# A top-k attention and channel-mix kernel: keys and queries stored as head, d, token

## The chip, the core and the metric

The kernel runs on one NeuronCore of a Trainium2 chip. The core has TensorE (PE: matmuls and transposes; its weight loads are listed as PEld), VectorE (DVE), ScalarE (ACT), GpSimd (POOL) and SyncE (SP, which here only issues DMAs). Each engine works through its own list of instructions in order and waits on semaphores for the others. Matmul results land in PSUM; everything else lies in SBUF, which, like PSUM, has 128 partitions. The metric is the device time of one launch in microseconds.

## The reference

Attention over 8 batches, 8 heads, 576 tokens and a head width of 64, in float32, in which each query keeps only its 32 largest scores; then a channel mix over the joined heads (512 channels, 1024 hidden).

```python
scores = scale * np.matmul(q, k.transpose(0, 1, 3, 2))
kth = np.partition(scores, -top_k, axis=-1)[..., -top_k:-top_k + 1]
mask = scores >= kth
scores = np.where(mask, scores, -1000000000.0)
scores = scores - np.max(scores, axis=-1, keepdims=True)
attn = np.exp(scores)
attn = attn / (np.sum(attn, axis=-1, keepdims=True) + 1e-09)
x = np.matmul(attn, v)              # then batch, token, head * d
...
xk = mu_k * x + (1.0 - mu_k) * x_prev
xr = mu_r * x + (1.0 - mu_r) * x_prev
k = np.maximum(xk @ w_k, 0.0)
v = k * k @ w_v
r = 1.0 / (1.0 + np.exp(-(xr @ w_r)))
return (r * v).astype(np.float32)
```

`x_prev` is x shifted by one token within its batch.

## The kernel before

**Tiles and slots.** Two heads make a pair; there are 4 pairs in each of 8 batches. A tile is 128 queries of one head against all 576 keys, the keys in two halves of 288 that stand on the upper and the lower 64 partitions of the key tile `K`. A pair of heads has 9 tiles: for each of four blocks of 128 tokens one tile per head, and a ninth for the last 64 tokens of both heads. A batch is walked in two halves: tiles 0 to 3 of the pairs 0, 1, 2, 3, then tiles 4 to 8 of the pairs 3, 2, 1, 0. Each such walk through a pair is a visit; there are 64 visits and 288 tiles. The key tile of a pair is made on its first visit and kept in one of four homes (`K0` to `K3`) for the second.

`pipeline` emits the program slot by slot, one tile entering in each. A slot n computes the scores of tile n (`scores`, L237, into the PSUM tile `ps`) and copies them to SBUF (`keep`, ACT, L246). One slot later DVE takes the eight largest of each of seven pieces of the row (`candidates`, L270), then the best of these in three rounds (L273, L276). ACT counts the scores over the 24th best (`count`, L286), POOL blanks those (`below`, L289), DVE takes the next eight (L915) and picks the 32nd value (L294). ACT computes the exponentials (L297), DVE masks and sums them (L300), TensorE turns the result (`turn_tile`, L313), ACT copies it (L317), and at the end of every four tiles TensorE multiplies it with v (`weigh`, L365) and DVE places the quotient into x (`place`, L371, L376). The steps of one slot come in the fixed order of the list `ORDER` (L42); a step's place there is its place in each engine's queue.

**Keys and queries before.** In DRAM they lie as batch, head, token, d. TensorE needs them with d on the partitions. So for each head j of a pair `load_keys` brings the keys as 96 tokens x 3 blocks x 2 halves (L178), `turn_k` transposes the three blocks into a PSUM tile (L206) and ACT copies it into `K` one slot later (L214, the place "high", second in the order). Queries come 256 tokens at a time (`load_near`, L172), each twice, so that they stand on both halves of the partitions after the turn; `turn_q` transposes the two blocks and ACT copies them (L209; DVE in the first pair, L221). The last 64 tokens of both heads go the same way through `load_rest` (L185), `turn_rest` and L227. All these PSUM tiles come from the pool `psM` (4 buffers), which the turned tiles and the channel mix use too. Keys are loaded 5 and 4 slots before the pair's first tile, queries 4 and 3 before it, and the turns are in the step `prep`, 4 to 1 slots before it. The first pair has its own `prep_first`, with a step `second` for its second head.

SP issues all DMAs in program order: weights (L120), keys, queries, v (L193, L194: these wait until the last products with the previous v are done) and the finished rows (L467).

**Channel mix.** `mix_steps` hands out the channel mix in pieces, of 3 matmuls with 512 columns or 6 with 256 (`three`, L424 to L426: values are split in a high and a low part). A planner (`Lanes`) decides how many pieces a slot takes: TensorE's account gets `TENSOR` at the end of each slot (L609, not over `CAP`), the attention's steps charge it (0.92 for scores, 0.47 for the turn of a tile, 2.5 for `weigh`, 0.35 for each turn of keys or queries, L859 and L863), and each piece costs `PIECE`. The pieces wait for tokens to be complete, and in the first 215 us also for the weights, which are split into two parts by ACT, DVE and POOL. These numbers only order the program; nothing waits on them on the chip.

A second way through the kernel, `prep_all` and the loop over batches at L976, runs only if a check of the counts fails; it does not run here.

```python
PACE, TENSOR, SHARE, PIECE, CAP, MOST = 4.60, 4.10, 0.74, 0.71, 4.45, 4
...
self.free[lane] = min(self.free[lane] + (TENSOR if lane == "pe" else PACE), CAP)
```

Of the kernel before, what the change touches and what calls it, by code (L numbers as in the profile page):

```python
# [9 lines left out]
F32 = mybir.dt.float32  # L10
# [15 lines left out]
KB, KP = 3, 96  # L26
# [12 lines left out]
PACE, TENSOR, SHARE, PIECE, CAP, MOST = 4.60, 4.10, 0.74, 0.71, 4.45, 4  # L39
END, HASTE = 36, 0.56  # L40
EXPS, EVAC = 3, (0, 'et')
ORDER = """exp high norm evac best0 c0 drop0 c1 best1 c2 drop1 first score turn inv loads keep sign c3 best2 c4 bounds eighth norm2 count et late below act c5 early thr c6 second mask place mix prep weigh dve pool weights""".split()  # L42
# [3 lines left out]
def topk_attention_channel_mix(ctx: ExitStack, tc: tile.TileContext, q, k, v, mu_k, mu_r, w_k, w_v, w_r, out):  # L46
# [112 lines left out]
    def heads(x, batch, hp):  # L159
        return batch(x)[2 * hp:2 * hp + 2]  # L160

    def load_part(g, x, batch, hp, j, tag=None):
        t = g.one.tile([128, NKC, 2, D], F32, name="kq", tag=tag or f"kq{j}")
        for i in range(2):
            nc.sync.dma_start(t[:, :, i, :], heads(x, batch, hp)[j, :MAIN].rearrange("(p c) d -> p c d", c=NKC))
        return t

    def load_near(g, x, batch, hp, j, c0):

        t = g.one.tile([128, 2, 2, D], F32, name="q_near", tag=f"kq{j}")  # L170
        for i in range(2):
            nc.sync.dma_start(t[:, :, i, :], heads(x, batch, hp)[j, c0 * 128:(c0 + 2) * 128].rearrange("(c p) d -> p c d", p=128))  # L172
        return t

    def load_keys(g, batch, hp, j):
        t = g.one.tile([KP, KB, 2, D], F32, name=f"kt{j}")
        for i in range(2):
            nc.sync.dma_start(t[:, :, i, :], heads(k, batch, hp)[j, i * HS:(i + 1) * HS].rearrange("(b p) d -> p b d", p=KP))  # L178
        return t

    def load_rest(g, batch, hp):
        t = g.one.tile([128, 1, 2, D], F32, name="qr_in")
        for j in range(2):
            for i in range(2):
                nc.sync.dma_start(t[j * 64:(j + 1) * 64, 0, i, :], heads(q, batch, hp)[j, MAIN:])  # L185
        return t
# [9 lines left out]
    def flat(ap):  # L196
        return ap.rearrange("p e d -> p (e d)")

    def new_k(g, P):
        P.K = g.one.tile([128, 2, HS], F32, name="K", tag=f"K{P.home}")  # L200

    def turn(pt, x):

        n = x.shape[0]
        for c in range(x.shape[1]):
            nc.tensor.transpose(pt[:, c * n:(c + 1) * n], flat(x[:, c]), ident[:n, :n])  # L206

    def copy_out(fast):
        return nc.vector.tensor_copy if fast else lambda to, x: nc.scalar.activation(to, x, AF.Copy)  # L209

    def turn_k(g, P, j, L):
        pt = g.psM.tile([128, MAIN], F32, name="pk", tag="pm")[:, :HS]
        turn(pt, P.kt[j])
        L.at(1, "high", lambda: nc.scalar.activation(P.K[:, j], pt, AF.Copy))  # L214

    def turn_q(g, P, j, L, fast=False):
        n = P.qt[j].shape[1] * 128
        pt = g.psM.tile([128, MAIN], F32, name="pq", tag="pm")[:, :n]
        turn(pt, P.qt[j])
        P.qs[j] = g.one.tile([128, n], F32, name=f"qs{j}")  # L220
        L.at(1, "high", lambda: copy_out(fast)(P.qs[j], pt))  # L221

    def turn_rest(g, P, L):
        pt = g.psM.tile([128, MAIN], F32, name="pr", tag="pm")[:, :128]
        turn(pt, P.rest)
        P.qr = g.two.tile([128, 128], F32, name="qr")
        L.at(1, "high", lambda: nc.scalar.activation(P.qr, pt, AF.Copy))  # L227

# [3 lines left out]
    def scores(g, P, i):  # L232
        hs = [slice(e * 64, (e + 1) * 64) for e in range(2)]
        if i < 2 * NKC:
            c, j = divmod(i - P.first, 2)
            for e, h in enumerate(hs):
                nc.tensor.matmul(g.ps[:, e], lhsT=P.qs[j][h, c * 128:(c + 1) * 128], rhs=P.K[h, j], start=True, stop=True)  # L237
        else:
            for j in range(2):
                for e, h in enumerate(hs):  # L240
                    nc.tensor.matmul(g.ps[hs[j], e], lhsT=P.qr[h, hs[j]], rhs=P.K[h, j], start=True, stop=True)
        return g.ps
# [124 lines left out]
    def place(U):  # L367
        xT, hp = U.xT, U.P.hp
        if U.u < 2 and U.P.near:
            x = xT[:, hp, 1 + U.u * 256:1 + (U.u + 1) * 256].rearrange("p (u q) -> p u q", u=2)  # L370
            nc.vector.tensor_mul(x, U.pa, U.ri.rearrange("p (u q) -> p u q", u=2))  # L371
        elif U.u < 2:
            x = xT[:, hp, 1:1 + MAIN].rearrange("p (q c) -> p c q", c=NKC)[:, 2 * U.u:2 * U.u + 2, :]
            nc.vector.tensor_mul(x, U.pa, U.ri.rearrange("p (c q) -> p c q", c=2))
        else:
            nc.vector.tensor_mul(xT[:, hp, 1 + MAIN:], U.pa, U.ri[:, :64])  # L376
# [262 lines left out]
    def prep_all(g, P, batch, hp, L):  # L639
        P.first, P.near, P.home, P.qs = 0, False, 0, {}  # L640
        new_k(g, P)
        P.rest = load_rest(g, batch, hp)
        P.kt, P.qt = [], []
        load_v(g, P, batch, hp)
        for j in range(2):
            P.kt.append(load_keys(g, batch, hp, j))
            turn_k(g, P, j, L)
            P.qt.append(load_part(g, q, batch, hp, j))
            turn_q(g, P, j, L)
        turn_rest(g, P, L)  # L650

    def prep_first(g, P, batch, hp):

        L = Direct()
        new_k(g, P)
        P.kt = [load_keys(g, batch, hp, 0)]
        P.qt = [load_near(g, q, batch, hp, 0, 0)]
        P.kt.append(load_keys(g, batch, hp, 1))
        P.qt.append(load_near(g, q, batch, hp, 1, 0))
        load_v(g, P, batch, hp)  # L660

        def half(j):
            turn_k(g, P, j, L)
            turn_q(g, P, j, L, True)
        half(0)
        return lambda: half(1)
# [6 lines left out]
    def pipeline(g):  # L673
# [81 lines left out]
        def new_pair(n):  # L755
            P = Ps[n] = Env()
            P.n = n
            P.b, P.hp, P.part = visits[n]
            P.first, P.near, P.qs = P.part[0], len(P.part) < 9, {}
# [16 lines left out]
        other = prep_first(g, P, P.batch, P.hp)  # L776
# [3 lines left out]
        while n < total + 7 or "next" in state or L.busy():  # L780
# [5 lines left out]
            def loads():  # L786
                for N, t in coming(n):
                    early = N.n > 1
                    if N.own and (t == -5 or t == -4 and not early):
                        N.kt = [load_keys(g, N.batch, N.hp, 0)]  # L790
                    if t == -4:
                        N.qt = []
                        if N.own:
                            N.kt.append(load_keys(g, N.batch, N.hp, 1))
                        if 8 in N.part:
                            N.rest = load_rest(g, N.batch, N.hp)
                    if t in ((-4, -3) if early else (-3, -2)):
                        N.qt.append(load_near(g, q, N.batch, N.hp, len(N.qt), N.first // 2))
# [38 lines left out]
            def second():  # L837
                if n == 0:
                    other()

# [103 lines left out]
            do = dict(loads=loads, second=second, score=score, turn=turn_, inv=inv, exp=exp, weigh=weigh_, prep=prep, norm=norm, norm2=norm2, bounds=bounds_,  # L944
# [30 lines left out]
    with tc.If(again > 0):  # L975
        with tc.For_i(0, B, 1) as b, ExitStack() as stack:  # L976
# [5 lines left out]
            for hp in range(HP):  # L982
                P = Env()
                P.hp = hp
                prep_all(g, P, lambda x: x[bass.ds(b, 1)].rearrange("o h s d -> (o h) s d"), hp, L)
# [51 lines left out]
```

## Time and profile before

| | |
|---|---|
| median of 3 runs | 1322.38 us (1321.73 to 1330.58) |
| the profiled execution | 1321.01 us |
| its span in the profile | 1319.2 us |
| mean granted TensorE clock | 0.95 |
| DMA | 67.16 MB by SP's queue in 204720 packets, 20.4% of 16 engines' span |
| scores of the first tile start | 5.8 us |
| scores of the last tile start | 1209.2 us |

The profile is one execution, recorded by the hardware. Its page gives the busy time of each engine and the chain of work that ended last, followed back from the end. Groups gather the instructions of one line, engine and shape, with their count, busy time in us and mean in ns, and the idle time of the engine just before them with what ended it. The view by stretches gives the busy time of each engine between two times; "x" is the number of instructions. The view of waits lists who waited for whom: us in total, how many times, the longest. The timeline lists instructions by start, with their time in us; in brackets is the idle time before. Matmuls are pipelined, so their recorded times overlap.

### The profile page before, as it was taken

Reading aid. Unit: us, or ns where it says so; the run is one execution under the profiler, and the core shown is the slowest. Engines: PE = TensorE matmul, PEld = TensorE weight load, DVE = VectorE, ACT = ScalarE, POOL = GpSimd, SP = SyncE. Lnnn points to the kernel's source line nnn. Section 1 sums busy time; section 2 is a strip of 40 time slices with the busy share of each in tenths; the row PEclk is TensorE's granted clock in tenths of the full one; section 3 lists DMA queues with packets and bytes.
Section 4 is the critical chain, followed back from the end, with each engine's and each line's share of the span. In section 5 each row is a group of like instructions: output and inputs, shape, how many; then the busy total and the mean of one; then the engine's idle time right before and its main releaser. Section 6 shows DMA issues by size and latency. Waiting matters only on the chain.

```text
span 1319.2 us, 34927 instructions
## 1 busy us (share of the span) xinstructions
PE 1181.2 (90%) x11157; PEld 939.8 (71%) x11157; DVE 1128.6 (86%) x6388; ACT 1107.9 (84%) x2716; POOL 907.0 (69%) x837
## 2 busy tenths in 40 slices
PE   5756786899989899799989999999999999999997
PEld 3434564676867688577867787878787787778786
DVE  6999988888998999889998999999999898898100
ACT  5778886889998899898989999999999898898431
POOL 3768887668656866786658776778676758677662
PEclk9766888899999999899989999999999999999999
DMA  4232232211321122112221132122212221111000
GB/s 108 81 93 72 75 94 55 51 33 35 75 63 33 34 63 69 37 37 66 54 58 31 37 75 54 42 55 50 62 43 53 51 59 42 46 40 28 13 17 23
DMA packets 204912, 69.48 MB, mean 53 GB/s; under 512 B 197552, under 2 KB 197552, under 8 KB 204720
## 3 DMA queue, kind: packets, MB, share of 16 engines
q1 hardware_dynamic: 204720, 67.16, 20.4%
q8 instruction: 91, 1.49, 0.5%
q14 instruction: 101, 0.83, 0.2%
HBM read 57.68 MB, written 9.44 MB: 51 GB/s over the span
## 4 chain that ended last, share of the span: by engine, by line
PE 56%; DVE 16%; ACT 15%; POOL 9%; issue 2%; SPq 0%; DMA 0%; ACTq 0%; DVEq 0%; POOLq 0%
PE ps L365 10%; PE ps L237 8%; PE ph L424 5%; PE ph L425 4%; PE ph L426 4%; PE pv L424 4%; PE pt L313 4%; PE pv L426 4%; PE pv L425 3%; DVE cand L270 3%; ACT sc L246 3%; ACT sg L286 3%; DVE E L300 3%; POOL sg L289 3%; DVE top L915 2%; PE pz L424 2%
## 5 line engine op out<-in xcount | busy, mean ns | idle before, releaser
L289 POOL TENSOR_TENSOR sg<-sc,sg 128x576 f32<-128x576 f32 x288 | 410.5, 1425 | 283.2 <-ACT sg L286 277.5
L270 DVE MAX8 cand<-sc 128x8 f32<-128x82 f32 (+1 forms) x2016 | 468.3, 233 | 1.4 <-ACT sc L246 0.9
L915 DVE MAX8 top<-sg 128x8 f32<-128x576 f32 x288 | 217.7, 756 | 40.6 <-POOL sg L289 39.0
L246 ACT ACTIVATE sc<-ps 128x576 f32<-128x576 f32 x288 | 188.9, 656 | 71.2 <-PE ps L237 44.1
L286 ACT ACTIVATE sg<-sc,seen 128x576 f32<-128x576 f32 x288 | 224.5, 780 | 16.1 <-DVE seen L281 14.8
L237 PE MATMUL ps<-K,qs 64*128 64x288 f32 x1024 | 206.8, 483 | 32.8 <-DVE xT L371 15.3
L300 DVE SCALAR_TENSOR_TENSOR E<-sc,seen,se 128x576 f32<-128x576 f32 x288 | 231.8, 805 | 0.6 <-DVE cand L270 0.3
L297 ACT ACTIVATE se<-sc,seen 128x576 f32<-128x576 f32 x288 | 218.7, 759 | 3.6 <-DVE E L300 3.5
L317 ACT ACTIVATE et<-pt 128x320 f32<-128x320 f32 x576 | 219.7, 441 | 0.7 <-PE pt L338 0.7
L313 PEld LDWEIGHTS pt<-ident,E 64*128 64x128 f32 x2880 | 140.8, 145 | 103.6 <-issue 17.1
L365 PE MATMUL ps<-et,v_in 128*64 128x128 f32 (+1 forms) x2560 | 176.4, 285 | 28.1 <-ACT sc L246 19.4
L313 PE MATMUL pt<-ident,E 64*128 64x64 f32 x2880 | 151.2, 232 | 34.2 <-DVE E L300 19.6
L365 PEld LDWEIGHTS ps<-et,v_in 128*64 128x64 f32 x2560 | 146.2, 149 | 48.9 <-ACT sc L246 33.3
L424 PE MATMUL ph<-xh,wk 128*128 128x256 f32 (+2 forms) x608 | 178.9, 294 | 0.4 <-ACT qs L209 0.2
L273 DVE MAX8 top<-cand 128x8 f32<-128x56 f32 x864 | 177.2, 205 | 0.1
L425 PE MATMUL ph<-xl,wk 128*128 128x256 f32 (+2 forms) x608 | 170.8, 281 | 0.0
L426 PE MATMUL ph<-xh,wk 128*128 128x256 f32 (+2 forms) x608 | 170.6, 281 | 0.0
L237 PEld LDWEIGHTS ps<-K,qs 64*128 64x128 f32 x1024 | 81.8, 195 | 81.8 <-ACT sc L246 20.8
L425 PE MATMUL pv<-wv,hh 128*128 128x512 f32 (+1 forms) x296 | 118.1, 399 | 10.7 <-POOL wv L151 10.7
L426 PE MATMUL pv<-wv,hl 128*128 128x512 f32 (+1 forms) x296 | 118.8, 401 | 7.9 <-POOL hl L445 7.9
L424 PE MATMUL pv<-wv,hh 128*128 128x512 f32 (+1 forms) x296 | 125.1, 423 | 0.0
L424 PEld LDWEIGHTS ph<-xh,wk 128*128 128x128 f32 x608 | 116.0, 191 | 5.7 <-ACT qs L209 0.4
(91 smaller groups left out, 2474.9 us busy)
## 6 DMA issues: line engine op xcount, KB each, us to landing
q_near<-in_q SPq DMA_DIRECT2D x256, 64.0 KB, 2.1
v_in<-in_v SPq DMA_DIRECT2D x128, 128.0 KB, 2.5
kt<-in_k SPq DMA_DIRECT2D x128, 72.0 KB, 2.2
out<-eb SPq DMA_DIRECT2D x35, 256.0 KB, 2.1
early<-in_moe_w_k SPq DMA_DIRECT2D x8, 512.0 KB, 3.7
early<-in_moe_w_v SPq DMA_DIRECT2D x8, 512.0 KB, 3.4
vr_in<-in_v SPq DMA_DIRECT2D x64, 32.0 KB, 2.3
early<-in_moe_w_r SPq DMA_DIRECT2D x4, 512.0 KB, 3.5
```

The lines of the kernel that those rows point to most:

```text
L237: nc.tensor.matmul(g.ps[:, e], lhsT=P.qs[j][h, c * 128:(c + 1) * 128], rhs=P.K[h, j], start=True, stop=True)
L246: nc.scalar.activation(T.sc.rearrange("p (e k) -> p e k", e=2), T.ps, AF.Copy)
L270: nc.vector.max(T.cand[:, 8 * i:8 * i + 8], T.sc[:, CUTS[i]:CUTS[i + 1]])
L286: nc.scalar.activation(T.side, T.sc, AF.Sign, bias=T.under, scale=-BELOW, accum_out=T.cnt)
L289: nc.gpsimd.tensor_mul(T.side, T.sc, T.side)
L300: nc.vector.scalar_tensor_tensor(T.e, T.sc, T.thr, g.pe, op0=OP.is_ge, op1=OP.mult, accum_out=T.rs)
L313: nc.tensor.transpose(pt[:, c * 64:(c + 1) * 64], T.e[h, k0:k0 + 128], ident[h, h])
L365: nc.tensor.matmul(pa[hs[j]], lhsT=lhsT, rhs=ms[c][j], start=(c == 0), stop=(c == NKC))
L424: nc.tensor.matmul(ps, lhsT=sh, rhs=mh, start=first, stop=False)
L425: nc.tensor.matmul(ps, lhsT=sh, rhs=ml, start=False, stop=False)
L426: nc.tensor.matmul(ps, lhsT=sl, rhs=mh, start=False, stop=last)
L915: nc.vector.max(M.top[:, 24:32], M.side)
```

## The change

The arrays of keys and queries are handed to the kernel as batch, head, d, token; the host orders them so before the launch, outside the measured time. The key tile and the query tile are now written by the DMAs as the scores' matmuls read them: two DMAs for the keys of a pair (one for each half of the keys, 64 partitions x 2 heads x 288 tokens) and two for the queries of a visit (the same queries to both halves of the partitions, 64 partitions x 2 heads x 256 or 320 tokens). The query tile has two buffers; the last 64 tokens are part of it. Keys are loaded 5 slots ahead (4 for the second pair), queries 4 (3). The turns, their copies, and the steps `prep` and `second` are gone, and with them their charges to the planner. `TENSOR` is 3.90 instead of 4.10.

```diff
-KB, KP = 3, 96
-PACE, TENSOR, SHARE, PIECE, CAP, MOST = 4.60, 4.10, 0.74, 0.71, 4.45, 4
+PACE, TENSOR, SHARE, PIECE, CAP, MOST = 4.60, 3.90, 0.74, 0.71, 4.45, 4
...
-    def load_part(g, x, batch, hp, j, tag=None):
...
-    def load_near(g, x, batch, hp, j, c0):
...
-    def load_rest(g, batch, hp):
...
+    def load_keys(g, P, batch, hp):
+        P.K = g.one.tile([128, 2, HS], F32, name="K", tag=f"K{P.home}")
         for i in range(2):
+            nc.sync.dma_start(P.K[i * 64:(i + 1) * 64], heads(k, batch, hp)[:, :, i * HS:(i + 1) * HS].rearrange("h d s -> d h s"))
+
+    def load_queries(g, P, batch, hp, c0, c1):
+        P.c0 = c0
+        P.qs = g.two.tile([128, 2, c1 - c0], F32, name="qs")
+        for i in range(2):
+            nc.sync.dma_start(P.qs[i * 64:(i + 1) * 64], heads(q, batch, hp)[:, :, c0:c1].rearrange("h d s -> d h s"))
...
-    def turn_k(g, P, j, L):
...
-    def turn_q(g, P, j, L, fast=False):
...
-    def turn_rest(g, P, L):
...
-            c, j = divmod(i - P.first, 2)
+            c, j = divmod(i, 2)
+            x = c * 128 - P.c0
             for e, h in enumerate(hs):
-                nc.tensor.matmul(g.ps[:, e], lhsT=P.qs[j][h, c * 128:(c + 1) * 128], rhs=P.K[h, j], start=True, stop=True)
+                nc.tensor.matmul(g.ps[:, e], lhsT=P.qs[h, j, x:x + 128], rhs=P.K[h, j], start=True, stop=True)
...
+                    if N.own and t == (-5 if early else -4):
+                        load_keys(g, N, N.batch, N.hp)
+                    if t == (-4 if early else -3):
+                        load_queries(g, N, N.batch, N.hp, N.c0, N.c1)
...
-            def prep():
-                for N, t in coming(n):
-                    at = (-4, -3) if N.n > 1 else (-3, -2)
-                    if N.own and t == at[0]:
-                        new_k(g, N)
-                    if N.own and t in at:
-                        turn_k(g, N, at.index(t), L)
-                        L.use("pe", 0.35)
-                        L.use("act", 0.4)
-                    if t in (-2, -1):
-                        turn_q(g, N, t + 2, L)
-                        L.use("pe", 0.35)
-                        L.use("act", 0.4)
-                    if t == 0 and 8 in N.part:
-                        turn_rest(g, N, L)
...
+        if name in ("q", "k"):
+            a = a.transpose(0, 1, 3, 2)
```

More of the change, by code (lines that the diff above doesn't have):

```diff
@@ L38 @@
 NEG = -3.0e38
-PACE, TENSOR, SHARE, PIECE, CAP, MOST = 4.60, 4.10, 0.74, 0.71, 4.45, 4
+PACE, TENSOR, SHARE, PIECE, CAP, MOST = 4.60, 3.90, 0.74, 0.71, 4.45, 4
 END, HASTE = 36, 0.56
 EXPS, EVAC = 3, (0, 'et')
-ORDER = """exp high norm evac best0 c0 drop0 c1 best1 c2 drop1 first score turn inv loads keep sign c3 best2 c4 bounds eighth norm2 count et late below act c5 early thr c6 second mask place mix prep weigh dve pool weights""".split()
+ORDER = """exp high norm evac best0 c0 drop0 c1 best1 c2 drop1 first score turn inv loads keep sign c3 best2 c4 bounds eighth norm2 count et late below act c5 early thr c6 mask place mix weigh dve pool weights""".split()
 @with_exitstack
@@ L160, in heads @@
         return batch(x)[2 * hp:2 * hp + 2]
-    def load_part(g, x, batch, hp, j, tag=None):
-        t = g.one.tile([128, NKC, 2, D], F32, name="kq", tag=tag or f"kq{j}")
+    def load_keys(g, P, batch, hp):
+        P.K = g.one.tile([128, 2, HS], F32, name="K", tag=f"K{P.home}")
         for i in range(2):
-            nc.sync.dma_start(t[:, :, i, :], heads(x, batch, hp)[j, :MAIN].rearrange("(p c) d -> p c d", c=NKC))
-        return t
-    def load_near(g, x, batch, hp, j, c0):
-        t = g.one.tile([128, 2, 2, D], F32, name="q_near", tag=f"kq{j}")
+            nc.sync.dma_start(P.K[i * 64:(i + 1) * 64], heads(k, batch, hp)[:, :, i * HS:(i + 1) * HS].rearrange("h d s -> d h s"))
+    def load_queries(g, P, batch, hp, c0, c1):
+        P.c0 = c0
+        P.qs = g.two.tile([128, 2, c1 - c0], F32, name="qs")
         for i in range(2):
[L172 to L179, printed above, removed]
-    def load_rest(g, batch, hp):
[L182 to L186, printed above, removed]
+            nc.sync.dma_start(P.qs[i * 64:(i + 1) * 64], heads(q, batch, hp)[:, :, c0:c1].rearrange("h d s -> d h s"))
     def load_v(g, P, batch, hp):
@@ L194, in load_v @@
         nc.sync.dma_start(P.vr[64:], h[:, MAIN:].rearrange("h p d -> p h d"))
[L196 to L209, printed above, removed]
-    def turn_k(g, P, j, L):
-        pt = g.psM.tile([128, MAIN], F32, name="pk", tag="pm")[:, :HS]
-        turn(pt, P.kt[j])
-        L.at(1, "high", lambda: nc.scalar.activation(P.K[:, j], pt, AF.Copy))
-    def turn_q(g, P, j, L, fast=False):
[L217 to L221, printed above, removed]
-    def turn_rest(g, P, L):
[L224 to L227, printed above, removed]
     class Tile_:
@@ L234, in scores @@
         if i < 2 * NKC:
-            c, j = divmod(i - P.first, 2)
+            c, j = divmod(i, 2)
+            x = c * 128 - P.c0
             for e, h in enumerate(hs):
-                nc.tensor.matmul(g.ps[:, e], lhsT=P.qs[j][h, c * 128:(c + 1) * 128], rhs=P.K[h, j], start=True, stop=True)
+                nc.tensor.matmul(g.ps[:, e], lhsT=P.qs[h, j, x:x + 128], rhs=P.K[h, j], start=True, stop=True)
         else:
+            x = MAIN - P.c0
             for j in range(2):
                 for e, h in enumerate(hs):
-                    nc.tensor.matmul(g.ps[hs[j], e], lhsT=P.qr[h, hs[j]], rhs=P.K[h, j], start=True, stop=True)
+                    nc.tensor.matmul(g.ps[hs[j], e], lhsT=P.qs[h, j, x:x + 64], rhs=P.K[h, j], start=True, stop=True)
         return g.ps
@@ L368, in place @@
         xT, hp = U.xT, U.P.hp
-        if U.u < 2 and U.P.near:
+        if U.u < 2:
             x = xT[:, hp, 1 + U.u * 256:1 + (U.u + 1) * 256].rearrange("p (u q) -> p u q", u=2)
             nc.vector.tensor_mul(x, U.pa, U.ri.rearrange("p (u q) -> p u q", u=2))
-        elif U.u < 2:
-            x = xT[:, hp, 1:1 + MAIN].rearrange("p (q c) -> p c q", c=NKC)[:, 2 * U.u:2 * U.u + 2, :]
-            nc.vector.tensor_mul(x, U.pa, U.ri.rearrange("p (c q) -> p c q", c=2))
         else:
@@ L637, in spans, with prep @@
         return pieces
[L639 to L643, printed above, removed]
-        load_v(g, P, batch, hp)
[L645 to L666, printed above, removed]
+    def prep(g, P, batch, hp, c0, c1):
+        load_keys(g, P, batch, hp)
+        load_queries(g, P, batch, hp, c0, c1)
+        load_v(g, P, batch, hp)
     def new_batch(g, b=0):
@@ L758, in new_pair @@
             P.b, P.hp, P.part = visits[n]
-            P.first, P.near, P.qs = P.part[0], len(P.part) < 9, {}
+            P.first = P.part[0]
+            P.c0, P.c1 = P.first // 2 * 128, S if 8 in P.part else (P.part[-1] + 1) // 2 * 128
             P.last = n % HP == HP - 1
@@ L775, in pipeline @@
         P = new_pair(0)
-        other = prep_first(g, P, P.batch, P.hp)
+        prep(g, P, P.batch, P.hp, P.c0, P.c1)
         load_mu()
@@ L788, in loads @@
                     early = N.n > 1
[L789 to L798, printed above, removed]
+                    if N.own and t == (-5 if early else -4):
+                        load_keys(g, N, N.batch, N.hp)
+                    if t == (-4 if early else -3):
+                        load_queries(g, N, N.batch, N.hp, N.c0, N.c1)
                     if t == 5:
@@ L835, in inv @@
                     L.use("act", 0.25)
-            def second():
-                if n == 0:
-                    other()
             def exp():
@@ L942, in place_ @@
                     nc.vector.tensor_reduce(least[:, V.P.n // HP:V.P.n // HP + 1], V.P.group[:, :, 1:, o], axis=mybir.AxisListType.XYZ, op=OP.min)
-            do = dict(loads=loads, second=second, score=score, turn=turn_, inv=inv, exp=exp, weigh=weigh_, prep=prep, norm=norm, norm2=norm2, bounds=bounds_,
+            do = dict(loads=loads, score=score, turn=turn_, inv=inv, exp=exp, weigh=weigh_, norm=norm, norm2=norm2, bounds=bounds_,
                       count=count_, below=below_, keep=keep_, mix=mix, eighth=eighth, thr=thr, mask=mask_, place=place_, weights=weights)
@@ L983, in topk_attention_channel_mix @@
                 P = Env()
-                P.hp = hp
-                prep_all(g, P, lambda x: x[bass.ds(b, 1)].rearrange("o h s d -> (o h) s d"), hp, L)
+                P.hp, P.home = hp, 0
+                prep(g, P, lambda x: x[bass.ds(b, 1)].rearrange("o h s d -> (o h) s d"), hp, 0, S)
                 for i in range(9):
@@ L1026 @@
     for name in _INS:
-        a = np.ascontiguousarray(inputs[name])
+        a = np.asarray(inputs[name])
+        if name in ("q", "k"):
+            a = a.transpose(0, 1, 3, 2)
+        a = np.ascontiguousarray(a)
         if a.dtype == np.float64:
```

## The prediction

> **What bounds the kernel now.** I read the page first: the busy shares, then the chain that ended last.
>
> ```profile
> span 1319.2 us, 34927 instructions
> PE 1181.2 (90%) x11157; PEld 939.8 (71%) x11157; DVE 1128.6 (86%) x6388; ACT 1107.9 (84%) x2716; POOL 907.0 (69%) x837
> PE 56%; DVE 16%; ACT 15%; POOL 9%; issue 2%; SPq 0%; DMA 0%; ACTq 0%; DVEq 0%; POOLq 0%
> ```
>
> No DMA is on the chain, and three engines lie within six points of each other, so an average says little. The next view is the table of busy time by stretches, cut where the work changes: three stretches in which the weights are still split into two parts, the steady stage, which begins and ends at a copy of scores, and the tail after the last tile's copy.
>
> ```profile
> core 0: us, PE busy (x) PEld busy (x) DVE busy (x) ACT busy (x) POOL busy (x), PEclk, DMA share, GB/s
> 12.40:92.10 79.70, 51.20 (x374) 33.43 (x376) 77.82 (x378) 62.06 (x142) 50.60 (x41) 0.82 0.33 89
> 92.10:189.70 97.60, 69.29 (x636) 52.66 (x634) 88.99 (x437) 80.21 (x190) 83.80 (x74) 0.76 0.27 77
> 189.70:277.70 88.00, 68.86 (x594) 53.36 (x590) 75.25 (x409) 68.41 (x165) 56.93 (x50) 0.86 0.23 57
> 277.70:1210.10 932.40, 886.46 (x8859) 714.40 (x8857) 868.00 (x5094) 854.98 (x2126) 660.24 (x607) 0.99 0.21 50
> 1210.10:1319.20 109.10, 99.55 (x697) 82.88 (x693) 16.25 (x62) 38.79 (x93) 54.48 (x60) 0.97 0.06 19
> ```
>
> From 12 to 92 us DVE works 77.8 of 79.7 us: it is the limit there, and TensorE's share does not matter. In the steady stage (932 us, 233 tiles, 4.00 us a tile) TensorE is busy 886, DVE 868, ACT 855: TensorE is first, but DVE stands only 18 us behind it. In the tail TensorE is alone. So the change can gain in the steady stage what lies between TensorE and DVE, and beyond that only what DVE now waits.
>
> **What the change removes, and its cost.** The work removed, from the groups by line over the whole run:
>
> ```profile
> L206 PE MATMUL pq<-ident,q_near 128*128 128x128 f32 x256 | 54.3, 296 | 8.9 <-ACT qs L209 5.1 <-DVE early L132 2.1 <-DMA q_near<-in_q 0.6
> L206 PE MATMUL pk<-ident,kt 96*128 96x96 f32 x192 | 29.0, 262 | 4.8 <-DMA kt<-in_k 3.5 <-ACT K L214 1.3
> L206 PE MATMUL pr<-ident,qr_in 128*128 128x128 f32 x32 | 9.0, 280 | 0.9 <-ACT qs L209 0.9
> L209 ACT ACTIVATE qs<-pq 128x256 f32<-128x256 f32 x126 | 49.7, 395 | 9.9 <-PE pq L206 9.0
> L214 ACT ACTIVATE K<-pk 128x288 f32<-128x288 f32 x64 | 26.6, 416 | 15.9 <-PE pk L206 14.6
> L227 ACT ACTIVATE qr<-pr 128x128 f32<-128x128 f32 x32 | 9.3, 291 | 8.8 <-PE pr L206 8.7
> ```
>
> ACT loses 49.7 + 26.6 + 9.3 = 85.6 us. TensorE's 92.3 us overlap their neighbours, so what they really take is read from starts in the timeline:
>
> ```profile
> 377.38 0.39 PE L425 MATMUL pv<-wv,hh 128*128 128x512 f32 x1
> ...
> 377.61 0.39 PE L426 MATMUL pv<-wv,hl 128*128 128x512 f32 x1
> ...
> 377.85 0.38 PE L206 MATMUL pq<-ident,q_near 128*128 128x128 f32 x2
> ...
> 378.15 0.30 PEld L237 LDWEIGHTS ps<-K,qs 64*128 64x128 f32 x4 [0.17 <-issue]
> ...
> 379.42 0.41 PE L206 MATMUL pk<-ident,kt 96*128 96x96 f32 x3
> ...
> 379.76 0.31 PEld L365 LDWEIGHTS ps<-et,v_in 128*64 128x64 f32 x6
> ```
>
> Two query transposes hold the engine from 377.85 to 378.15, 0.30 us; three key transposes from 379.42 to 379.76, 0.34. That is 128 x 0.30 + 64 x 0.34 + 32 x 0.15 (one transpose of the rest, half of a pair) = 38.4 + 21.8 + 4.8 = 65 us at most, since the 0.17 of issue before the scores may stay; without it for the 128 query turns, 65 - 21.8 = 43. I take the middle, 54 us, of which the steady stage holds
>
> ```profile
> 277.70:1210.10 932.40, 67.16 (x375) 45.93 (x375) 0.99 0.21 50
> ```
>
> 375 of 480 transposes (the row counts line 206 on PE and PEld): 0.78 x 54 = 42 us. ACT's part there is 0.78 x 85.6 = 67 us.
>
> **What it moves.** `TENSOR` falls from 4.10 to 3.90. A tile's budget was also charged for the transposes: per nine tiles two key and four query turns of 0.35, 0.23 a tile. So the pieces of the channel mix get 3.90 against 4.10 - 0.23 = 3.87: 0.03 a tile more. That is 233 x 0.03 = 7 us of mix that leaves the tail for the steady stage. In the tail TensorE does 99.55 of 109.10 us, nearly all matmuls of the mix, so it ends up to 7 us earlier; where the mix starves for tokens a larger budget is lost, so the bounds are 0 and 10.
>
> **Steady stage.** TensorE: 886 - 42 + 7 = 851 us. ACT: 855 - 67 = 788. DVE: 868 as before; nothing is taken from it but two copies at the start. DVE becomes the first engine, and the stage cannot fall under 868. What DVE waits for today, by the view of waits in this stage:
>
> ```profile
> DVE top L915 <- POOL sg L289: 32.7, 79, 1.3
> DVE rs L327 <- ACT rs L323: 12.7, 19, 1.1
> PEld pt L313 <- ACT qs L209: 6.6, 12, 1.5
> PEld pq L206 <- ACT qs L209: 5.3, 9, 0.9
> POOL sg L289 <- ACT sg L286: 220.0, 153, 3.6
> ```
>
> DVE idles 932 - 868 = 64 us: 32.7 for POOL's product, which itself waits for ACT's count (220.0), and 12.7 for ACT directly. Both begin with ACT, which gets 67 / 233 = 0.29 us a tile back, taken from places ahead of the copy of the scores and the count. I let ACT's 12.7 and a good third of POOL's go: 64 to 39. So the stage is 868 + 39 = 907, a gain of 25. The ends: 8 us if DVE keeps nearly all its waits (56 of 64 stay), and 50 if TensorE's 42 - 7 = 35 go in full with some 12 us of its waits for ACT's query copies (6.6 + 5.3) and a few more: 882, where DVE would be 98% busy, as it is from 12 to 92 us.
>
> From 92 to 278 us DVE is busy 164 of 186, so 21 us is the most there; of ACT's copies and TensorE's turns 480 - 375 = 105 transposes lie before the steady stage, some 60 of them here: 11 and 7 us. A quarter of DVE's idle time, 5 us; bounds 0 and 10. From 12 to 92 us nothing: 2 us are left.
>
> **The start.** DVE's first candidates wait for the mu vectors, whose DMAs stand behind eleven others on SP, and then for the second query copy.
>
> ```profile
> 9.74 0.17 DVE L92 TENSOR_SCALAR nmu<-mu 128x8 f32<-128x8 f32 x1 [4.06 <-DMA mu<-in_moe_mu_r]
> ...
> 10.15 1.11 DVE L270 MAX8 cand<-sc 128x8 f32<-128x82 f32 x7
> ```
>
> Keys and queries of the first pair become 4 DMAs instead of 8. An issue takes SP about 0.5 us (two in 0.91 to 0.98 in the timeline's SP rows), so mu lands 2 us earlier, and the copy that lies between these two rows goes: 2.4, say 2.5 us; bounds 1 and 3.5. The first scores don't stand in the way: the fourth DMA is issued by 2.7 us, and with the 2.5 to 3.7 to landing of the rows below the scores start at 5.2 to 6.4 and their copy ends some 2 us later, so near the upper end it is they that hold the first candidates, and the gain is 1.
>
> **The DMAs that take over.** 64 key DMAs of 144 KB and 128 query DMAs of 128 or 160 KB replace 512 smaller ones. Nearest rows:
>
> ```profile
> v_in<-in_v SPq DMA_DIRECT2D x128, 128.0 KB, 2.5
> early<-in_moe_w_k SPq DMA_DIRECT2D x8, 512.0 KB, 3.7
> SPq L193 <- PE ps L365: 543.0, 58, 15.7
> ```
>
> So 2.5 to 3.7 us to landing, near 2.5. They are costed at nothing because the steady loads are issued five (keys) and four (queries) tiles ahead, 16 us at 4.00 a tile. The cover goes only if SP, which issues in order, stands at another wait: the loads of v wait for the last weighing, 543 us in 58 waits, up to 15.7. But a load of v at tile 5 of a pair asks for a weighing of tile 4, which is done a tile before, and the two query buffers ask only for the scores of the pair before the last, done as early; so a load behind them leaves about when its place in the order says. If the cover is gone, each first score of 64 visits is late by what is missing.
>
> **The sum.** Start 2.5, to 278 us 5, steady 25, tail 7: 39.5 us. The profiled execution took 1321.0 (span 1319.2 and 1.8 around it), 1.4 under the median of 1322.4. 1321.0 - 39.5 = 1281.5; I say 1282.
>
> **The rivals.**
> TensorE's time comes back in full: steady 50, tail 10, to 278 us 7, start 2.5: 1321 - 69.5 = 1251.5. For it: TensorE is on 56% of the chain. Against it: DVE would have to run at 98% for 882 us.
>
> The loops hold the steady stage: each tile goes from score to copy to candidates to count to mask to transpose, and DVE keeps its 64 us of waits. Then start 2.5, tail 7 and 2 before 278 us remain: 1321 - 11.5 = 1309.5. For it: DVE at 93% and POOL's wait of 220 us behind ACT's count, of which the transposes are no part. Against it: ACT's copies stand ahead of that count on its queue. The Trainium skill, Perfetto Trace Analysis, section Identifying the Most-Contended Engine, points this way: it holds matmul busy time to be a bad measure and asks for the share of weight loads. By that rule TensorE stands at 714 of 932 us here, 77%, behind DVE and ACT, and taking its work away frees nothing. The trace speaks half against it: in the timeline above matmuls of 0.39 us start 0.23 apart without a gap.
>
> Slower, by the clock: TensorE gets idle stretches, and its granted clock falls with them.
>
> ```profile
> 264.00:330.00 66.00, 60.03 (x609) 48.11 (x611) 58.66 (x346) 59.17 (x147) 49.70 (x50) 0.97 0.14 34
> ```
>
> In the stretch from 190 to 278 us, above, it is 0.86. At that clock the remaining 851 us become 851 x 0.99 / 0.86 = 980, with today's 46 us of idle time 1026: 93 us worse in the stage, 1321 + 93 - 14.5 = 1400. It decides once 851 x 0.99 / c passes 886, below c = 0.95. Against it: 0.86 comes with TensorE busy 78% (68.86 of 88.00); I expect 94% (851 of 907), and the row with 91% has 0.97, where 851 becomes 869, about DVE's 868. The Trainium skill, TensorE: Matmul & The Clock Gate, section Part 1, has the same direction: the clock halves after an idle window of about 3.4 us. The longest waits of TensorE quoted here are 1.5 us.
>
> **How the numbers follow.** The forecast 0.56 (its own range 1265 to 1298), TensorE in full 0.19, the loops 0.20, slower by clock or late loads 0.05. The 1282 is the forecast's. The range: from 1246, which leaves out a quarter of the second case (0.05), to 1309, which leaves out half of the third (0.10) and the slower one (0.05): 0.2 in all. About 1% is what a measurement of this kernel can tell from no change: 1309 to 1336. Faster: 0.56 + 0.19 + 0.10 of the loops' case = 0.85; within 1%: the other 0.10 and 0.01 of the slower case; slower 0.04.
>
> **What would show it.** Right: no line 206, 209, 214 or 227; ACT about 85 us lower; DVE's busy time the same within 5 us, its share in the steady stage up from 93% to about 95.5%, and above TensorE's; the steady stage near 907 us; DVE's wait for POOL's product near 20 us; the tail at 99 to 105; the first candidates near 8 us. Wrong: scores that wait for a DMA of keys or queries; a granted clock under 0.95 in the steady stage; DVE's share unmoved; or a tail that grew, which would mean that the smaller budget, not the transposes, set the pace of the mix.

## The result

| | before | changed |
|---|---|---|
| median | 1326.5 us (4 runs, 1321.7 to 1330.9) | 1292.1 us (4 runs, 1291.0 to 1294.0) |
| ratio | | 0.974, 95% interval 0.970 to 0.979 |
| the profiled execution | 1321.0 us | 1291.7 us |
| its span | 1319.2 us | 1289.9 us |

The changed kernel is 2.6% faster. The kernel before measured 1319 to 1334 us over all the chips used below, in two groups, near 1322 us at a granted clock of 0.95 and 1328 to 1334 us at 0.93 to 0.945, and its one profile is of the first group. So kernels are compared by their ratio to it on the same chip, and by the lengths of their stages in the profiles, one profile each. A stage is always cut at the same copies of scores (of tile 54 and of the last tile).

The page of the changed kernel, the rows that answer to those of before:

```profile
span 1289.9 us, 33246 instructions
PE 1126.9 (87%) x10677; PEld 884.2 (69%) x10677; DVE 1125.0 (87%) x6386; ACT 1047.1 (81%) x2494; POOL 905.4 (70%) x837
PE 48%; DVE 23%; POOL 13%; ACT 11%; issue 3%; SPq 1%; DMA 0%; DVEq 0%; ACTq 0%; POOLq 0%
qs<-in_q SPq DMA_DIRECT2D x64, 160.0 KB, 3.0
K<-in_k SPq DMA_DIRECT2D x64, 144.0 KB, 2.9
```

TensorE lost 54 us of busy time and ACT 61; DVE lost 4 and POOL 2. A part of the chain has gone from TensorE and ACT to DVE and POOL; DMAs have 0% of it, as before. Next the busy time by stretches, in the changed kernel: the steady stage and the tail.

```profile
core 0: us, PE busy (x) PEld busy (x) DVE busy (x) ACT busy (x) POOL busy (x), PEclk, DMA share, GB/s
270.90:1181.60 910.70, 851.84 (x8483) 674.49 (x8480) 863.95 (x5093) 806.29 (x1949) 658.86 (x607) 0.98 0.19 50
1181.60:1289.90 108.30, 99.31 (x699) 83.07 (x695) 16.24 (x63) 39.14 (x93) 54.56 (x60) 0.98 0.06 19
```

The steady stage is 910.7 us instead of 932.4, the tail 108.3 instead of 109.1, and what lies before the steady stage 270.9 instead of 277.7. So the 29.3 us of the profiled executions are 6.8 + 21.7 + 0.8.

What DVE, and what TensorE, waited for in the steady stage of the changed kernel:

```profile
POOL sg L242 <- ACT sg L239: 199.3, 134, 3.2
PEld ps L318 <- ACT sc L199: 40.0, 52, 2.1
DVE top L816 <- POOL sg L242: 28.6, 71, 1.2
PE ps L318 <- ACT sc L199: 26.9, 42, 1.8
DVE rs L280 <- ACT rs L276: 5.6, 11, 0.7
```

The rows of before for TensorE's wait:

```profile
PEld ps L365 <- ACT sc L246: 24.5, 46, 2.4
PE ps L365 <- ACT sc L246: 13.7, 16, 2.1
```

POOL waits 21 us less for ACT's count, DVE 4 less for POOL and 7 less for ACT. TensorE now waits more at the products with v (line 318, line 365 before) for the copy of the slot's scores: 26.9 against 13.7 us. A part of the time taken from it came back as waiting.

### The profile page after: what moved, and what is told of

It reads as the page before. It is cut to its first block, busy times and chain, and to the rows that moved or that the text cites. A ratio compares the mean times of both kernels' runs of the same rounds, so it can differ in the third digit from the quotient of the medians.

```text
span 1289.9 us, 33246 instructions
## 1 busy us (share of the span) xinstructions
PE 1126.9 (87%) x10677; PEld 884.2 (69%) x10677; DVE 1125.0 (87%) x6386; ACT 1047.1 (81%) x2494; POOL 905.4 (70%) x837
## 2 busy tenths in 40 slices
DMA packets 113767, 69.35 MB, mean 54 GB/s; under 512 B 81840, under 2 KB 106416, under 8 KB 113584
## 3 DMA queue, kind: packets, MB, share of 16 engines
q1 hardware_dynamic: 113584, 67.14, 19.0%
## 4 chain that ended last, share of the span: by engine, by line
PE 48%; DVE 23%; POOL 13%; ACT 11%; issue 3%; SPq 1%; DMA 0%; DVEq 0%; ACTq 0%; POOLq 0%
PE ps L318 9%; PE ps L189 7%; POOL sg L242 5%; DVE cand L223 5%; DVE top L816 4%; DVE E L253 4%; PE ph L374 4%; PE pv L374 4%; PE ph L375 4%; PE pv L376 4%; PE ph L376 3%; PE pt L266 3%; ACT sc L199 3%; PE pv L375 3%; POOL xl L370 2%
## 5 line engine op out<-in xcount | busy, mean ns | idle before, releaser
L189 PE MATMUL ps<-K,qs 64*128 64x288 f32 x1024 | 211.1, 489 | 54.1 <-ACT sc L199 24.4
L239 ACT ACTIVATE sg<-sc,seen 128x576 f32<-128x576 f32 x288 | 223.7, 777 | 23.1 <-DVE seen L234 20.4
L266 PE MATMUL pt<-ident,E 64*128 64x64 f32 x2880 | 148.0, 232 | 33.7 <-DVE E L253 19.0
L374 PE MATMUL pv<-wv,hh 128*128 128x512 f32 (+1 forms) x296 | 127.2, 430 | 0.0
L375 PE MATMUL pv<-wv,hh 128*128 128x512 f32 (+1 forms) x296 | 119.0, 402 | 7.6 <-POOL wv L150 7.6
```

The costliest lines, as they stand in the source:

```text
L189: nc.tensor.matmul(g.ps[:, e], lhsT=P.qs[h, j, x:x + 128], rhs=P.K[h, j], start=True, stop=True)
L239: nc.scalar.activation(T.side, T.sc, AF.Sign, bias=T.under, scale=-BELOW, accum_out=T.cnt)
L266: nc.tensor.transpose(pt[:, c * 64:(c + 1) * 64], T.e[h, k0:k0 + 128], ident[h, h])
L374: nc.tensor.matmul(ps, lhsT=sh, rhs=mh, start=first, stop=False)
L375: nc.tensor.matmul(ps, lhsT=sh, rhs=ml, start=False, stop=False)
```

## The experiments

### Which part of the removed work mattered

The change does three things: it takes 480 transposes from TensorE and 222 copies from ACT (375 and 177 of them in the steady stage), and it gives the planner another budget. First the planner alone: e1 is the changed kernel with the old budget and the old charges, so that the pieces of the mix are handed out by the old account.

```diff
-PACE, TENSOR, SHARE, PIECE, CAP, MOST = 4.60, 3.90, 0.74, 0.71, 4.45, 4
+PACE, TENSOR, SHARE, PIECE, CAP, MOST = 4.60, 4.10, 0.74, 0.71, 4.45, 4
...
+            def prep_():
+                for N, t in coming(n):
+                    at = (-4, -3) if N.n > 1 else (-3, -2)
+                    if N.own and t in at:
+                        L.use("pe", 0.35)
+                        L.use("act", 0.4)
+                    if t in (-2, -1):
+                        L.use("pe", 0.35)
+                        L.use("act", 0.4)
...
```

> The changed kernel with the planner of the kernel before: TENSOR 4.10, and each turn that is no longer there still charged 0.35 to TensorE and 0.4 to ACT. Theory A (the gain is the work taken off TensorE and ACT; the smaller budget moves nothing, since both kernels had handed out 616 of 748 pieces at the last tile): 1290 to 1294 us, steady stage within 4 us of 911. Theory B (the planner's constants bring part of the gain): 1298 us or more.

Measured: 1300.8 us, ratio 0.979 (0.975 to 0.983), steady stage 917.0 us, the tail 109.1. This is over Theory B's bound of 1298, with 6 us more in the steady stage than with 3.90. The intervals of the two ratios overlap, so that the budget brought something is likely, not certain. The tail says that it was not by moving pieces out of it.

e2 and e3 put the two kinds of work back, one each, on top of e1.

```diff
...
+                        pd = g.psM.tile([128, MAIN], F32, name="pd", tag="pm")
+                        for c in range(3):
+                            nc.tensor.transpose(pd[:, c * 96:(c + 1) * 96], ident[:96], ident[:96, :96])
...
```

> As e1, with TensorE's 480 transposes put back where they were, of the identity instead of keys and queries, so that nothing waits for a DMA and no copy follows. Theory A1 (TensorE's time was the larger part: with its 42 us back it is again first in the steady stage, 894 against DVE's 864): steady stage 922 to 932, 1305 to 1317 us. Theory A2 (ACT's copies were the larger part, ahead of the scores' copy and the count on its queue): steady stage under 918, under 1301 us.

```diff
...
+                        L.at(1, "high", lambda: nc.scalar.activation(scrap[:, :288], plain[:, :288], AF.Copy))
...
```

> As e1, with ACT's copies put back in their place in the order (288, 256 and 128 columns, from a constant tile in SBUF to a scratch tile, so nothing waits). Theory A1: steady stage under 918 and under 1301 us, since TensorE at 852 and DVE at 864 still have room. Theory A2: 922 to 932, 1305 to 1317 us. If both e2 and e3 come near 1322, each alone is enough to bring the old time, and the gain needs both.

Measured: e2 1318.7 us, ratio 0.992 (0.990 to 0.994); e3 1317.8 us, ratio 0.992 (0.989 to 0.996). The steady stages, e2 first, then e3, in the columns of the tables above:

```profile
275.30:1207.40 932.10, 892.78 (x8859) 723.18 (x8855) 865.69 (x5094) 804.84 (x1949) 659.87 (x607) 0.97 0.18 49
```

```profile
274.20:1206.90 932.70, 862.11 (x8483) 685.34 (x8480) 866.14 (x5096) 858.32 (x2125) 659.30 (x606) 0.96 0.18 49
```

The two rows differ in the engine that carries the load (TensorE 893 and ACT 805, or TensorE 862 and ACT 858) and not in length: 932.1 and 932.7, against 917.0 in e1. So each part alone costs 15 to 16 us, and neither A1 nor A2 holds, by which one of them would have cost next to nothing.

That 932.4 was also the stage of before does not show that either part alone brings back the whole old time. The 932.4 come from an execution of 1321.0 us; on the chip of e1 to e3 the median of the kernel before was 1331.0 us, 12 to 13 us over e2 and e3, and both ratios lie under 1 with their intervals. By these medians the transposes add 17.9 us to e1 and the copies 17.0, and e1 is 30.2 under the kernel before.

The traces tell more. In each of them the granted clock is either 1.0 or 0.5, and how long it is 0.5 differs from trace to trace. Here is such a stretch in e1, with the 3.5 us before it, in the columns of the tables above:

```profile
377.90:381.40 3.50, 1.28 (x14) 0.72 (x14) 3.44 (x22) 2.34 (x7) 1.98 (x2) 1.00 0.50 160
381.40:391.60 10.20, 7.96 (x60) 6.18 (x62) 9.63 (x57) 8.31 (x21) 9.39 (x9) 0.50 0.02 5
```

The steady stage has 233 slots, from the start of one copy of scores to the next. In 205 of them the clock is 1.0 throughout in all five traces:

| | before | changed | e1 | e2 | e3 |
|---|---|---|---|---|---|
| those 205 slots, us | 805.9 | 790.1 | 782.2 | 796.9 | 792.5 |
| the other 28, us | 126.5 | 120.6 | 134.8 | 135.2 | 140.2 |
| at clock 0.5 in the stage, us | 27 | 37 | 55 | 55 | 75 |

In the 205 slots the transposes cost 14.7 us over e1 and the copies 10.3; the kernel before, which has both, is 23.7 over e1. There the two parts nearly add up to the old length. TensorE is busy 794 of the 806 us there before the change, and 753 of 790 after it, where DVE is busy 752 too: the average of the whole stage (95% before) hides that TensorE was nearly full in most slots. The old budget of e1 is 7.9 us shorter there than 3.90 and loses 14.2 in the other 28 slots, so what 3.90 brings lies where some trace has clock 0.5. Whether the clock itself makes those slots long, or the idle time of TensorE ahead of it, no run separates.

e2 also takes turns in the PSUM pool `psM`, which e3 does not; the last pair of runs is about this pool.

### Whether an engine sets the pace now

After the change DVE is busy 864 of 910.7 us, TensorE 852, ACT 806. Three runs take time from one of them each.

```diff
-                    nc.vector.max(M.top[:, 24:32], M.side)
+                    nc.vector.max(M.top[:, 24:32], M.side[:, :HS])
```

> The changed kernel with the last of DVE's four rounds of eight looking at 288 of 576 columns, about 0.3 us less of DVE's time a tile, 70 us in the steady stage; the other half of the columns is left out of the ninth to sixteenth largest under the bound, so the output differs. Theory A (DVE is now the first engine and sets the pace): the steady stage falls by 20 to 40 us, until TensorE at 852 holds it; 1250 to 1273 us. Theory C (the loop from scores to copy to count and back holds it, no engine alone): by 8 to 20 us. Theory G (TensorE still sets the pace): under 8 us.

```diff
-            three(ph[:, e, :n], wk[0][:, h, w], wk[1][:, h, w], xh[:, h, :n], xl[:, h, :n], h == 0, h == HP - 1)
+            two(ph[:, e, :n], wk[0][:, h, w], wk[1][:, h, w], xh[:, h, :n], xl[:, h, :n], h == 0, h == HP - 1)
```

> The changed kernel without the third product (low part by high part) of the hidden layer, 608 matmuls of some 0.12 us, about 54 us of TensorE's time in the steady stage and 13 us in the tail; the output differs by that product. Theory A: the steady stage falls by less than 10 us, the tail by 10 to 13; 1268 to 1282 us. Theory C: the steady stage by 8 to 20 us. Theory G: by 30 us or more, 1250 us or less.

```diff
-        nc.scalar.activation(g.pe, T.sc, AF.Exp, bias=T.nb, scale=SCALE)
+        w = HS if getattr(g, "filled", False) else S
+        g.filled = True
+        nc.scalar.activation(g.pe[:, :w], T.sc[:, :w], AF.Exp, bias=T.nb, scale=SCALE)
```

> The changed kernel with ACT's exponentials over 288 of 576 columns from the second tile on, about 0.3 us less of ACT's time a tile, 70 us in the steady stage; the other half keeps the values of the first tile, so the output differs. Theory A: the steady stage falls by less than 10 us, 1282 us or more. Theory C: by 8 to 20 us.

And the three together:

> The three cuts at once: DVE's last round of eight over half the columns, ACT's exponentials over half, no third product of the hidden layer. One by one they took 6.5, 7.4 and 9.0 us from the steady stage, 23 in sum, for 62, 52 and 42 us of busy time. Theory C (waits in the loop hold the stage, engines only at the edge): about the sum, 880 to 893 us. Theory H (a slot is as long as its longest engine, a different one from slot to slot, so that one cut is covered by the other two): far more than the sum, 862 us or less.

| | busy time taken in the steady stage | steady stage | shorter by | whole run |
|---|---|---|---|---|
| changed kernel | | 910.7 us | | 1292.1 us |
| e6, DVE | 62 us | 904.2 | 6.5 | 1279.4 |
| e7, TensorE | 42 us | 901.8 | 8.9 | 1272.5 |
| e8, ACT | 52 us | 903.3 | 7.4 | 1282.1 |
| e10, all three | 50 + 65 + 57 = 172 us | 874.7 | 36.0 | 1239.4 |

The steady stages of e6 and e10:

```profile
264.40:1168.60 904.20, 849.28 (x8482) 672.83 (x8480) 801.59 (x5093) 803.44 (x1949) 659.46 (x607) 0.98 0.19 51
```

```profile
262.40:1137.10 874.70, 801.83 (x8026) 621.01 (x8024) 798.59 (x5094) 749.20 (x1948) 656.69 (x606) 0.98 0.20 52
```

A cut on one engine gives back between 10% and 21% of what it took. In e6 DVE is busy 89% and has its time still. So DVE, the busiest engine of the stage, does not set the pace alone: e6's 6.5 us rule out theory A (20 to 40), and e7's 8.9 rule out G (30 or more). C's 8 to 20 us hold for e7 alone; e6 and e8 fall short of them. All three together give 36 us, more than the sum of the single ones (23) and far less than what was cut: between C and H. With all three cut each engine is at or under 92%.

In the 204 slots in which none of these five traces has clock 0.5, the falls are 2.9 us for DVE's cut, 14.3 for TensorE's, 7.0 for ACT's and 36.0 for all three. There TensorE's cut is worth most and DVE's least, though DVE has the larger busy time in the stage. A likely reading, not shown, is that a tile passes from engine to engine and that the engine it waits for changes; which of the waits would have to go was not found. The other savings of e6 and e7 lie outside the steady stage: e6's early stages, in the first of which DVE is the limit, fell by 7 us, e7's tail by 10.

### The budget of the planner

e4 is the changed kernel with `TENSOR` 4.10 and no charges, e5 with 3.75.

> The changed kernel with TENSOR 4.10 and no charges for turns, so 0.2 us a tile more for the pieces of the mix. Theory A: the pieces wait for tokens, not for the budget, over most of the run; the same 616 pieces or up to 10 more at the last tile, 1284 to 1296 us. Theory B: more pieces in the slots, the tail shorter by 10 us or more and the steady stage longer by as much or more.

> The changed kernel with TENSOR 3.75. With 4.10 fourteen more pieces were done by the last tile and the tail was 9 us shorter, but the steady stage 34 us longer. Theory E (the length of a slot is the longest of the engines' shares in it, so pieces given in bursts cost more than their time): fewer pieces a slot are spread more evenly; steady stage 896 to 908 us, tail up to 15 us longer, 1286 to 1298 us in all. Theory F (the steady stage is DVE with its waits, whatever the pieces do at or under 3.90): steady stage within 4 us of 911, tail longer by what is left over, 1296 to 1306 us.

Measured: e4 1317.1 us, ratio 0.991 (0.987 to 0.994); e5 1289.9 us, ratio 0.972 (0.966 to 0.979). Steady stage and tail of each:

```profile
272.30:1216.60 944.30, 877.07 (x8548) 700.38 (x8546) 868.77 (x5100) 810.01 (x1954) 665.70 (x613) 0.96 0.18 49
1216.60:1315.80 99.20, 89.72 (x633) 74.23 (x629) 15.35 (x59) 35.75 (x87) 47.51 (x53) 0.98 0.07 21
```

```profile
271.20:1169.10 897.90, 835.75 (x8418) 661.22 (x8415) 860.74 (x5091) 801.48 (x1940) 649.95 (x599) 0.99 0.19 51
1169.10:1287.70 118.60, 109.04 (x765) 92.16 (x763) 17.22 (x65) 42.61 (x101) 62.65 (x69) 0.99 0.06 20
```

The tails differ by 66 matmuls of TensorE each way from the 699 of the changed kernel; counted by the mix's matmuls that is 14 pieces: about 10 us of TensorE's work. In the tail they cost that, 9.1 less with 4.10 and 10.3 more with 3.75. In the steady stage 14 more cost 33.6 us and 14 fewer save 12.8. So the same budget that frees the tail takes more than three times as much from the steady stage. For e4 theory A falls, and B has the direction, with 9.1 us in the tail for its 10 or more. Theory E has the sign and the numbers of e5 (897.9, 1289.9); that pieces given in bursts are the reason was not tried by itself, and the clock has a part: it is 0.5 for 82 us of e4's stage, 37 of the changed kernel's and 17 of e5's. In 195 slots at clock 1.0 in these three traces and in e1's, e4 is 15.9 us longer than the changed kernel and e5 5.6 shorter, about half of the differences. e5 and the changed kernel can't be told apart in all (0.972 and 0.974).

### The wait for the scores' copy, and the PSUM pool

TensorE's largest wait in the steady stage is at the products with v, for the copy of the scores. e9 lays the PSUM tile out anew.

```diff
-        scored = p("psS", 1, space=PSUM).tile([128, 2, 512], F32, name="ps")
-        g.ps = scored[:, :, :HS]
-        g.sums = scored[:, :, HS:HS + 128], scored[:, 0, HS + 128:HS + 192]
+        scored = p("psS", 1, space=PSUM).tile([128, 1024], F32, name="ps")
+        g.ps = scored[:, 512 - HS:512 + HS].rearrange("p (e k) -> p e k", e=2)
+        g.sums = scored.rearrange("p (x c) -> p x c", c=128)[:, 0:8:7], scored[:, 128:192]
```

> The changed kernel with the PSUM tile of the scores laid out anew: scores in columns 224 to 800, contiguous over the two banks, and the sums of the products with v in columns 0 to 128 and 896 to 1024 (before: scores in the first 288 columns of each bank, sums behind them). Before and after the change all 96 groups of products with v begin after the scores' copy of their slot has ended, 0.05 us later in the median. Theory W (they wait because the copy's range, taken from first to last column, covers the sums; this wait in the loop from scores to copy to products to the next scores is what holds the steady stage, TensorE's waits for the copy there being 27 us): the products begin before the copy ends, those waits go, the steady stage falls by 10 to 27 us, 1264 to 1282 us. Theory X (the wait is for the bank, or is not what holds the stage): the steady stage stays within 4 us of 911.

Measured: 1291.8 us, ratio 0.969 (0.964 to 0.975), steady stage 911.5. Still none of the 96 groups of products began during a copy, and the wait is there as before:

```profile
PEld ps L318 <- ACT sc L199: 40.3, 52, 2.1
PE ps L318 <- ACT sc L199: 27.2, 43, 1.8
```

So X has the number, and the columns were not the reason. In e11 the sums have a bank of their own, taken from the pool `psM`; e12 only takes the bank away.

```diff
-        g.sums = scored[:, :, HS:HS + 128], scored[:, 0, HS + 128:HS + 192]
+        sums = p("psW", 1, space=PSUM).tile([128, 512], F32, name="pw")
+        g.sums = sums[:, :256].rearrange("p (u q) -> p u q", u=2), sums[:, 256:320]
...
-        g.psM = p("psM", 4, space=PSUM)
+        g.psM = p("psM", 3, space=PSUM)
```

> The changed kernel with the sums of the products with v in a PSUM bank of their own, taken from the pool that the transposes used before (four buffers there become three). To be read against e12, which has the three buffers alone. Theory W (the products' wait for the scores' copy holds the steady stage): products begin during a copy, TensorE's waits for it go, and the steady stage is 10 us or more under that of e12. Theory X (that wait only takes up time in which TensorE would wait elsewhere): within 5 us of e12.

> The changed kernel with three buffers instead of four in the PSUM pool of turned tiles and mix. Theory X: the pool has lost 288 of its takers' turns (two keys, four queries and the rest per pair), so three do with little loss: steady stage 911 to 925 us. Theory P (the freed PSUM buffers are a part of the gain): 930 us or more, the old time.

(The 288 in the second is a slip: 64 key, 128 query and 32 rest tiles are 224.) Measured: e11 1326.3 us, ratio 0.998 (0.994 to 1.001), steady stage 944.9; e12 1334.5 us, ratio 1.002 (1.000 to 1.005), steady stage 951.5, over P's bound. In e11 34 of the 96 groups began during a copy, and the wait is gone from the list. So it came from sharing a bank or a tile with the scores; e11 gives the sums both of their own, and no run separates the two. The Trainium skill, PSUM — Partial Sum Buffer, section PSUM bank collisions raise a hardware error, speaks for the bank: by it two engines must not be in one bank on the same partitions at once, whatever the columns, so that software has to keep them apart. The new place brought 6.6 us against e12: between the bounds of W and X, and waiting shows up elsewhere, ACT's for the scores above all (65.5 us in e12, 103.2 in e11). In e11, then in e12:

```profile
PEld pw L319 <- DVE xT L325: 13.5, 10, 3.1
ACT sc L200 <- PE ps L190: 103.2, 120, 3.0
```

```profile
PEld ph L374 <- ACT et L270: 22.0, 35, 1.2
PEld pt L266 <- ACT eb L407: 11.3, 9, 1.8
```

The larger result is e12's: one PSUM buffer fewer costs 40.8 us of the steady stage, more than the change gained. Its rows show how: the mix and the turned tiles wait for ACT to empty a buffer. Before the change 224 key and query tiles went through the four buffers of this pool, each until ACT's copy a slot later, and turned tiles and query turns waited for those copies (6.6 and 5.3 us in the prediction's rows). The change takes them out. That the freed buffers are a part of the gain is possible from e12, but not shown: e12 takes a buffer for the whole run, and e3, which takes none, lengthens the stage as much as e2, which takes turns.

## Why the prediction was right

**The whole.** 1282 was forecast, with 1246 to 1309 as the range; 1292.1 came, a gain of 29.3 us in the profiled executions against 39.5. By terms: the start and the stages to 278 us 6.8 against 2.5 + 5; the steady stage 21.7 against 25; the tail 0.8 against 7. The direction and the order of the terms came as forecast; that the steady term lies so near was in part luck, as the next paragraphs show.

**The step that was mis-sized: the tail.** The prediction charged the budget's 0.03 a tile to the tail, 7 us. Both kernels have 99 to 100 us of TensorE's work in the tail and the same counts there, so no piece moved. e4 and e5 show that a budget does move pieces, 14 for 0.15 to 0.2, but 0.03 moved none. What the budget likely did was in the steady stage (e1: 6 us, one profile each), where the prediction had it at nothing.

**The removed work.** TensorE's steady share was forecast at 851 and is 851.8, but that is luck: two terms cancel. The forecast took 42 us of transposes off and added 7 us of mix. No mix came, and TensorE's busy time in the stage fell by 34.6; the transposes alone are 37.8 by e2 against e1. That the whole run fell by the forecast 54 (1181.2 - 1126.9 = 54.3) has the same weakness: ahead of the steady stage it fell by 19 us, where 12 were forecast. ACT's 85.6 us were too much: its busy time fell by 60.8, 0.27 us a copy instead of the 0.39 recorded, and in the stage by 49 and not 67. Records of neighbouring instructions overlap on ACT as on TensorE, which can be seen in the starts, where TensorE's cost was read:

```profile
16.91 0.41 ACT L214 ACTIVATE K<-pk 128x288 f32<-128x288 f32 x1
17.20 0.39 ACT L209 ACTIVATE qs<-pq 128x256 f32<-128x256 f32 x1
17.47 0.67 ACT L246 ACTIVATE sc<-ps 128x576 f32<-128x576 f32 x1
```

**The steady stage: the right length for half a reason.** 907 was forecast and 910.7 came; DVE stands first in busy time, at 94.9% (95.5% forecast). Its waits fell from 64 to 47 us (39 forecast): those for ACT from 12.7 to 5.6 and not to nothing, those for POOL from 32.7 to 28.6 and not to about 20. But the reason given, that DVE then sets the pace, falls with e6: 62 us off DVE shorten the stage by 6.5. That ACT's copies hold up the loop, the prediction's other reason, fits e3, where they add 15.7 us; e2 shows as much for TensorE's transposes. Whether the place of the copies in ACT's queue matters was not tried.

**The rivals.** TensorE's time did not come back in full: 21.7 of 42. The loops' case, the stage unmoved, did not come either, though e6 to e8 fit its picture, in which no engine alone holds the stage, better than the forecast's. The rule set beside it (the share of weight loads, by which TensorE was third and its work would free nothing) gave the wrong answer for this stage: 22 us went, and e2's transposes alone bring 15 back. It is right in one thing: by e7, 42 us off TensorE are worth only 9 (14 in the slots at clock 1.0). The mean clock of the stage fell from 0.99 to 0.98 and not under 0.95. Still the rival by the clock touched something real: the time at clock 0.5 rose from 27 to 37 us. Its condition was judged by TensorE's average; in the traces each such stretch follows 3.4 us in which TensorE was busy 64% or less, and an average of 94% leaves room for those.

**The DMAs.** Costed at nothing, and rightly. They land after 2.8 to 3.0 us, within the 2.5 to 3.7 of the bounds. In the whole run TensorE's matmuls waited for them twice, by the view of waits (us in total, times, longest):

```profile
PE ps L189 <- DMA qs<-in_q: 6.0, 2, 5.2
```

The 5.2 us are the start of the run, before the first matmul; the other 0.8 us, at 240.5 us of the run, are the only later ones, so this sign of being wrong stayed away but for them. At the start the mu vectors came 1.4 us earlier and not 2, because the larger DMAs take SP 0.61 us to issue where the old ones took 0.47; the first candidates began at 8.43 us instead of 10.15, 1.7 us earlier and not 2.5.

## What to carry to other kernels

Where three engines stand over 88% in a loop that hands a tile from one to the next, no average share of busy time tells what an instruction is worth: here 38 us on TensorE or 51 on ACT, added alone, lengthened the stage by 15 to 16 us, while a cut on any one engine returned a tenth to a fifth of itself. So the price of a part is measured by putting it back alone, and the slots at clock 1.0 in all traces are compared by themselves: there the parts nearly added up, and TensorE, at 95% over the old stage, was 98.5% busy. When transposes leave TensorE, look also at the PSUM buffers and at the plan that was balanced around them: a budget 0.2 higher cost 33.6 us of the stage and one buffer fewer 40.8, each more than the 21.7 that the change gained.

## What the runs showed of the hardware

A DMA from DRAM into 64 partitions, in runs of 1152 bytes, landed about as fast as one into 128 partitions in runs of 256 bytes: 144 KB in 2.9 us against 128 KB in 2.6. The packets on SP's queue fell from 204720 to 113584 for the same 67 MB, and the share of the DMA engines only from 20.4% to 19.0%.

```profile
v_in<-in_v SPq DMA_DIRECT2D x128, 128.0 KB, 2.6
q1 hardware_dynamic: 113584, 67.14, 19.0%
```

The granted clock goes to 0.5 after a short poor stretch of TensorE, not a poor average. In the 14 traces it did so 121 times in the steady stages, for 3.4 us or a multiple of it, each time after 3.4 us in which TensorE was busy 18 to 64%. The e1 rows above, 1.28 of 3.50 us and then clock 0.5, are one of them.

TensorE's busy time grows when it waits more: e12 has the matmuls of the changed kernel, the same 37 us at clock 0.5, and 871.3 us of busy time in the steady stage against 851.8. The ends of matmuls are modelled in the profile, so this is a warning on the reading and not a cost.
